# A fused attention and two mixture layers on one core: another order for VectorE and ScalarE in the second MoE, another place for the input's sums and the shares in the first

## The chip, the cores and the metric

The program runs on one core of one Trainium2 chip. Five engines work side by side, each through its own list of instructions in order: TensorE (PE, with its weight loads as PEld), VectorE (DVE), ScalarE (ACT), GpSimd (POOL) and SyncE (SP, which issues most loads). They meet at semaphores. The metric is the device time of one execution in microseconds; lower is better.

## What is computed

Attention within clusters gives x of 1536 tokens by 512. A gated layer and then a mixture of four experts follow:

```python
def _moe_ref(x, w_gate, w_val, w_out):
    g = x @ w_gate                      # 512 x 1536
    return g * sigmoid(g) * (x @ w_val) @ w_out
def _moe2_ref(x, domain_probs, w1, w2):
    p = domain_probs / (domain_probs.sum(-1, keepdims=True) + 1e-09)
    for e in range(4):                  # w1[e]: 512 x 1024, w2[e]: 1024 x 512
        out += p[:, e:e + 1] * (np.maximum(x @ w1[e], 0.0) @ w2[e])
```

## The kernel before

All matrices stay in fp32 accuracy: each operand is split into a high and a low part, and a product is three matmuls (high by high, high by low, low by high). The instructions stand on every engine in the order in which the code issues them; no scheduler moves them.

The tokens form three blocks (`tb` 0, 1, 2) of 512. In both MoEs blocks 0 and 1 are multiplied by a scheme of seven products in place of eight, on sums of blocks of the input (`x_sums`) and of the weights (`block_sums`); block 2 is multiplied plainly. The hidden width is cut into chunks. A generator of side work (weight conversion, sums) advances by `step()`; `work(rate)` sets how far.

**First MoE.** Chunk (1,0) runs `up` (gate and value products, silu) and `down_pair`; chunks (1,1) to (1,10) run `up_fast`, and a `down_pair` after each second one. `weights1` is the side work: it converts weights (`conv`) and makes the sums of x (`x_sums(1)`), for which x of blocks 0 and 1 is first copied whole into `acc` (`x_whole`); `down_pair` of chunk (1,0) then writes its results over `acc`. In chunk (1,5) `share_rows` normalizes the probabilities on DVE (`shares`, L772 to L775).

**Second MoE.** Chunks (2,0) to (2,15), four per expert. (2,0) runs plainly; (2,1) to (2,14) run `up_seven` and `down_seven`, the last one `up_seven` and `down`. In `up_seven` PE fills banks: `pa`, `pb`, `pc` for blocks 0 and 1, `third(key, f)` for block 2. From them DVE and ACT make m1, u2, m5 and t21 (a sum on a full bank, then Relu times the token's share in `relu_p`), their high parts by ACT (`hi`, a cast), their low parts by DVE (`lo`, a subtraction), and the differences of the scheme, `ts[1]` to `ts[4]`, each again as high and low. h11, h12, h21, h22 are the hidden blocks; h12's place holds `ts[4]`. Block 2 passes `relu_l`: Relu into the high part on ACT, the low part on DVE.

In `down_seven` seven products go through two pairs of banks, u and q. A product either starts its pair anew or adds to it. After each, either DVE adds the bank to `acc` (`by_v`), or ACT copies it to a buffer `ev` and POOL issues a DMA that adds it to `acc` (`by_a`). Between them stand four products of block 2 (`last_block`), copied by ACT with the token's share. The first product is copied by ACT (L1120), and the third needs the emptied bank:

```python
product(u, raw, 0, b11, True, by_a(0, 0))        # L1131
product(q, sums, 0, ts[1], True, by_v(1, 1))
rest()                                           # rest of t21, ts[4]
last_block(0)
product(u, sums, 256, ts[2], False, by_v(0, 1))  # L1135
```

The `ev` buffers are five, used in turn, and ACT waits for the DMA that last read one. `share_load` fetches the next expert's shares by SP.

## Time and profile before

| | us |
|---|---|
| runs, median of 3 | 1105.49 (1102.17 to 1106.14) |
| the profiled execution | 1110.94 |
| its span | 1108.7 |
| PE busy | 1051.8 |
| DVE, ACT, POOL busy | 825.5, 623.4, 410.5 |

Attention fills about the first 270 us of the span, the first MoE the time to about 554, the second the rest. The times below are from the span's start. A matmul's row has its modelled duration; since matmuls overlap, the distance between two starts tells what one costs. A wait in brackets is idle time of that engine and the instruction that ended it.

### The profile page before, as it was taken

Reading aid. Unit: us, or ns where it says so; the run is one execution under the profiler, and the core shown is the slowest. Engines: PE = TensorE matmul, PEld = TensorE weight load, DVE = VectorE, ACT = ScalarE, POOL = GpSimd, SP = SyncE. Lnnn points to the kernel's source line nnn. Section 1 sums busy time; section 2 is a strip of 40 time slices with the busy share of each in tenths; the row PEclk is TensorE's granted clock in tenths of the full one; section 3 lists DMA queues with packets and bytes.
Section 4 is the critical chain, followed back from the end, with each engine's and each line's share of the span. In section 5 each row is a group of like instructions: output and inputs, shape, how many; then the busy total and the mean of one; then the engine's idle time right before and its main releaser. Section 6 shows DMA issues by size and latency. Waiting matters only on the chain.

```text
span 1108.7 us, 14805 instructions
## 1 busy us (share of the span) xinstructions
PE 1051.8 (95%) x5051; PEld 846.0 (76%) x5051; DVE 825.5 (74%) x1468; ACT 623.4 (56%) x1200; POOL 410.5 (37%) x455
## 2 busy tenths in 40 slices
PE   9999999999999998999999998889988899888998
PEld 6778888887877887888887776667776677666777
DVE  6788888896788778786776667766677665776665
ACT  6778787886575545554455454444545445444451
POOL 2757777642000010101012454445544444444530
PEclk7999999999999999999999999999999999999999
DMA  7687778432614452525001655446563366634652
GB/s 194 169 186 180 160 178 175 116 93 85 159 58 104 105 115 77 133 65 125 20 20 38 133 114 125 81 100 133 114 139 86 83 130 114 131 75 99 133 95 114
DMA packets 61267, 126.23 MB, mean 114 GB/s; under 512 B 15648, under 2 KB 20256, under 8 KB 61192
## 3 DMA queue, kind: packets, MB, share of 16 engines
q0 software_dynamic: 35632, 62.93, 30.7%
q1 hardware_dynamic: 25272, 62.30, 18.6%
q8 instruction: 39, 0.64, 0.2%
q14 instruction: 36, 0.29, 0.1%
q10 hardware_dynamic: 288, 0.07, 0.0%
HBM read 69.47 MB, written 3.21 MB: 66 GB/s over the span
## 4 chain that ended last, share of the span: by engine, by line
PE 71%; DVE 16%; ACT 6%; issue 3%; DMA 2%; POOL 0%; DVEq 0%; ACTq 0%; SPq 0%; POOLq 0%
PE pa L889 12%; PE pb L266 9%; PE pd L1223 8%; PE pd L1103 8%; PE ps L449 5%; PE pb L1153 4%; PE ps L426 4%; DVE snap L1008 3%; PE pb L889 3%; PE ps L427 3%; PE pa L266 2%; PE pv L479 2%; PE pv L484 2%; PE pc L361 2%; PE pv L485 2%
## 5 line engine op out<-in xcount | busy, mean ns | idle before, releaser
L432 DVE CUSTOM_DVE_ANT_0 junk<-ps,zero 128x768 bf16<-128x768 f32 x96 | 91.0, 947 | 15.6 <-PE ps L427 13.3
L194 POOL TENSOR_TENSOR ws<-wraw 128x256 f32<-128x256 f32 x29 | 35.8, 1235 | 170.7 <-issue 101.2
L1121 POOL DMA_DIRECT2D acc<-ev x84 | 74.4, 1026 | 65.8 <-ACT ev L1120 60.8
L1229 POOL DMA_DIRECT2D acc<-ev x24 | 20.7, 884 | 209.1 <-ACT ev L1228 204.5
L443 ACT ACTIVATE P<-ps,nm 128x768 f32<-128x768 f32 x96 | 86.6, 902 | 16.1 <-DVE nm L432 15.8
L1114 DVE TENSOR_TENSOR acc<-pd,acc 128x512 f32<-128x512 f32 x112 | 74.0, 686 | 19.7 <-PE pd L1103 19.4
L266 PE MATMUL pb<-xh,wuh 128*128 128x512 f32 x216 | 85.4, 396 | 0.0
L266 PE MATMUL pb<-xh,wul 128*128 128x512 f32 x216 | 84.9, 393 | 0.0
L266 PE MATMUL pb<-xl,wuh 128*128 128x512 f32 x216 | 84.1, 389 | 0.0
L449 PE MATMUL ps<-ident,P 128*128 128x128 f32 x576 | 82.7, 275 | 0.0
L468 DVE TENSOR_TENSOR lo<-ps,hi 128x384 fp32r<-128x384 f32 x128 | 69.3, 554 | 15.1 <-ACT hi L454 14.0
L426 PE MATMUL ps<-t 80*128 80x512 f32 x192 | 71.6, 373 | 1.0 <-ACT t L402 0.8
L1129 POOL DMA_DIRECT2D acc<-ev x56 | 50.1, 944 | 60.2 <-ACT ev L1128 46.5
L454 ACT CAST hi<-ps 128x384 fp32r<-128x384 f32 x128 | 57.3, 479 | 20.8 <-PE ps L449 20.4
L889 PE MATMUL pa<-xsh,wuh 128*128 128x512 f32 x150 | 61.2, 408 | 7.7 <-DVE snap L1005 7.4
L449 PEld LDWEIGHTS ps<-ident,P 128*128 128x128 f32 x576 | 65.5, 141 | 1.5 <-DVE lo L468 0.2
L1128 ACT ACTIVATE ev<-pb,pn 128x512 f32<-128x512 f32 x56 | 37.4, 686 | 48.3 <-DMA acc<-ev 35.6
L427 PE MATMUL ps<-t 128*128 128x512 f32 x192 | 63.1, 349 | 0.0
L889 PE MATMUL pa<-xh,wuh 128*128 128x512 f32 x150 | 58.6, 391 | 2.5 <-ACT snap L894 2.5
L889 PE MATMUL pa<-xsh,wul 128*128 128x512 f32 x150 | 59.0, 393 | 0.0
L889 PE MATMUL pa<-xsl,wuh 128*128 128x512 f32 x150 | 58.9, 393 | 0.0
L1223 PE MATMUL pd<-hh,wdh 128*128 128x512 f32 x144 | 56.8, 394 | 2.0 <-ACT acc L1225 2.0
(272 smaller groups left out, 3194.2 us busy)
## 6 DMA issues: line engine op xcount, KB each, us to landing
acc<-ev POOLq DMA_DIRECT2D x164, 256.0 KB, 4.9
wraw<-in_wm SPq DMA_DIRECT2D x68, 512.0 KB, 3.5
t<-in_qk POOLq DMA_DIRECT2D x13, 768.0 KB, 6.1
t<-in_qk POOLq DMA_DIRECT2D x14, 384.0 KB, 6.8
raw<-in_qk SPq DMA_DIRECT2D x26, 192.0 KB, 6.4
x<-x SPq DMA_DIRECT2D x21, 192.0 KB, 2.9
R<-rd SPq DMA_DIRECT2D x16, 192.0 KB, 3.5
out<-acc SPq DMA_DIRECT2D x11, 256.0 KB, 2.0
```

The costliest lines, as they stand in the source:

```text
L266: T.matmul(out=ps, lhsT=w[:, o:o + 128], rhs=x, start=(k == 0 and m == 0), stop=(k == 3 and m == 2))
L426: T.matmul(out=ps, lhsT=t2[:, 0, qs], rhs=t2[:, 1, ks], start=True, stop=False)
L427: T.matmul(out=ps, lhsT=t1[:, 0, qs], rhs=t1[:, 1, ks], start=False, stop=True)
L432: V.tensor_tensor_reduce(out=junk, in0=S_t[n], in1=zero1.to_broadcast([128, S]), scale=-0.125, scalar=3.0e38, op0=ALU.add, op1=ALU.min, ac ...
L443: A.activation(out=P_t[n], in_=S_t.pop(n), func=ACTF.Exp, scale=0.125, bias=nm_t.pop(n), accum_out=rs_t[p][:, h, c:c + 1])
L449: T.transpose(ps[:, i * 128:(i + 1) * 128], P_t[3 * u + i][:, j * 128:(j + 1) * 128], ident)
L468: V.tensor_tensor(out=lo, in0=ps, in1=hi.bitcast(F32), op=ALU.subtract)
L889: T.matmul(out=ps, lhsT=w[:, o:o + 128], rhs=r, start=first and i == 0 and m == 0, stop=i == 1 and m == 2, skip_group_check=not first)
L1103: T.matmul(out=ps[s], lhsT=w[i][:, o + s * 128:o + s * 128 + 128], rhs=x[j], start=first and m == 0, stop=m == 2, skip_group_check=not first)
L1114: V.tensor_tensor(out=y, in0=ps, in1=y, op=ALU.add)
L1121: G.dma_start(out=acc1[:, 2 * half + s, tb * 512:(tb + 1) * 512], in_=ev, accum_op=ALU.add)
L1223: T.matmul(out=ps, lhsT=w[:, o:o + 128], rhs=x[:, f, sl], start=(n == 0), stop=(n == len(terms) - 1))
```

## The change

In the second MoE, the DVE and ACT work of `up_seven` is issued in another order. DVE's sums on banks (`plus`) come ahead of the differences. The Relu of block 2's second half is split: its ACT part (`relu_h`) stays in `up_seven`, its DVE part (`relu_lo`) follows the second product of `down_seven`. t21 and its high part (`c21`) move there too, behind ACT's copies of the first product; the rest of t21 follows the third product. Three steps of side work come ahead of block 2's first half, and the last steps of `down_seven` go.

In the first MoE, the shares are made in chunk (1,0), from a tile that is loaded ahead of x; the sums of x come after two converted pieces of weights in place of four, and wait until block 1 of that chunk has been multiplied; `up` and `down_pair` of that chunk take the blocks in the order 0, 1, 2.

```diff
@@ share_rows
-            pt = ev_.tile([128, 128, E2], F32, tag="ev", name="pt")[0:NR]
-            SY.dma_start(out=pt, in_=probs_t)
-            yield
             shares(ct["pr"], prs[:, 0:NL], pn)
             yield
             to = ev_.tile([128, E2, 128], F32, tag="ev", name="po")[0:NR]
-            shares(pt, prs[0:NR], to.rearrange("t e n -> t n e"))
+            shares(ct["pt"], prs[0:NR], to.rearrange("t e n -> t n e"))
@@ relu_l is split
+        def relu_h(key, f, g):
+            A.activation(out=h_blk(key, f, 2)[0], in_=g, func=ACTF.Relu)
+
+        def relu_lo(key, f, g):
+            h = h_blk(key, f, 2)
+            V.scalar_tensor_tensor(out=h[1], in0=g, scalar=0.0, in1=h[0].bitcast(F32), op0=ALU.max, op1=ALU.subtract)
@@ up_seven
             prod(key, pa, S_(2), T_(2), False)
             u2 = snap(pa)
             lo(h11, m1)
+            for _ in range(3):
+                step()
             relu_l(key, 0, third(key, 0))
-            step()
             prod(key, pc, S_(4), B_(1, 1), False)
             plus(u2, pc, u2)
             relu_p(key, u2, u2, 1)
+            if not blocks:
+                hi(h12, u2)
+            prod(key, pa, S_(3), T_(3), False)
+            plus(m5, pa, m5)
+            relu_p(key, m5, m5, 1)
+            hi(h22, m5)
+            g = third(key, 1)
+            prod(key, pa, A_(1, 1), T_(4), False)
             if blocks:
                 ts[1] = [wp.tile([128, 512], F32R, tag="wb", name="th", bufs=2) for _ in range(2)]
                 minus(m1, u2, m1)
                 hi(ts[1], m1)
-                step()
-                lo(ts[1], m1)
-            else:
-                hi(h12, u2)
-                step()
-                lo(h12, u2)
-            prod(key, pa, S_(3), T_(3), False)
-            plus(m5, pa, m5)
-            relu_p(key, m5, m5, 1)
-            hi(h22, m5)
-            if blocks:
                 minus(u2, m5, u2)
                 hi(ts[3], u2)
                 lo(h22, m5)
                 minus(m5, m5, m1)
+                lo(ts[1], m1)
+                relu_h(key, 1, g)
                 hi(ts[2], m5)
-            else:
-                lo(h22, m5)
-            step()
-            relu_l(key, 1, third(key, 1))
-            if blocks:
                 lo(ts[2], m5)
                 lo(ts[3], u2)
-            prod(key, pa, A_(1, 1), T_(4), False)
...
-            relu_p(key, t21, pa, 0)
-            hi(h21, t21)
+
+            def c21():
+                relu_p(key, t21, pa, 0)
+                hi(h21, t21)
 
             def rest():
                 lo(h21, t21)
                 minus(t21, t21, m5)
                 hi(ts[4], t21)
+                step()
                 lo(ts[4], t21)
@@ down_seven
-            if (key[1] + 1) % NC2 == 0:
-                share_load(e + 1)
...
             product(u, raw, 0, b11, True, by_a(0, 0))
             product(q, sums, 0, ts[1], True, by_v(1, 1))
-            rest()
+            relu_lo(key, 1, g)
+            c21()
+            h_t.pop(key)
+            if (key[1] + 1) % NC2 == 0:
+                share_load(e + 1)
             last_block(0)
             product(u, sums, 256, ts[2], False, by_v(0, 1))
             step()
+            rest()
             product(q, sums, 768, b22, False, by_a(0, 1))
...
             product(q, raw, DM, b21, True, by_v(0, 0))
-            step()
             last_block(2)
             product(u, raw, DM + 256, ts[4], False, by_v(1, 0))
-            step()
             last_block(3)
@@ up
-            for tb in (0, 2, 1):
+            for tb in range(3):
...
+                        done.add((key, f, tb))
@@ down_pair
-            for tb in (1, 0, 2) if last else (2, 0, 1) if first else (1, 2, 0):
+            for tb in (1, 0, 2) if last else (0, 1, 2) if first else (1, 2, 0):
@@ weights1
-            yield from conv(todo[:4])
+            yield from conv(todo[:2])
+            yield from share_rows()
+            while (chunks[0], 1, 1) not in done:
+                yield
             yield from x_sums(1)
-            yield from conv(todo[4:])
+            yield from conv(todo[2:])
@@ the loop over chunks
+        ct["pt"] = ev_.tile([128, 128, E2], F32, tag="ev", name="pt")[0:NR]
+        SY.dma_start(out=ct["pt"], in_=probs_t)
         x_whole()
...
-                work(2.5)
+                work(3)
                 down_pair(k)
```

What this does to the order, at three places. First DVE, in chunk (2,3) of the second MoE, from the sum on the m5 bank (before: from the u2 bank). snap_7319 is u2, snap_7309 m5, snap_7277 m1, th is ts[1], wul holds the low parts of ts[2] and ts[3], pd are the down banks. Before:

```order
L1005 TENSOR_TENSOR snap_7319<-pa_7302,snap_7319 128x512
L996 SCALAR_TENSOR_TENSOR snap_7319<-snap_7319,pe_6288 128x512
L1008 TENSOR_TENSOR snap_7277<-snap_7319,snap_7277 128x512
L250 TENSOR_TENSOR wsl_7294<-ws_7295,wsh_7293 128x512
L1002 TENSOR_TENSOR th_7350<-snap_7277,th_7349 128x512
L1005 TENSOR_TENSOR snap_7309<-pa_7270,snap_7309 128x512
L996 SCALAR_TENSOR_TENSOR snap_7309<-snap_7309,pe_6288 128x512
L1008 TENSOR_TENSOR snap_7319<-snap_7309,snap_7319 128x512
L1002 TENSOR_TENSOR hl_7280<-snap_7309,hh_7279 128x512
L1008 TENSOR_TENSOR snap_7309<-snap_7309,snap_7277 128x512
L250 TENSOR_TENSOR wsl_7294<-ws_7296,wsh_7293 128x512
L1013 SCALAR_TENSOR_TENSOR hl_7280<-pb_7380,hh_7279 128x512
```

Now:

```order
L1002 TENSOR_TENSOR snap_7309<-pa_7270,snap_7309 128x512
L993 SCALAR_TENSOR_TENSOR snap_7309<-snap_7309,pe_6288 128x512
L1005 TENSOR_TENSOR snap_7277<-snap_7319,snap_7277 128x512
L1005 TENSOR_TENSOR snap_7319<-snap_7309,snap_7319 128x512
L999 TENSOR_TENSOR hl_7280<-snap_7309,hh_7279 128x512
L1005 TENSOR_TENSOR snap_7309<-snap_7309,snap_7277 128x512
L999 TENSOR_TENSOR th_7390<-snap_7277,th_7389 128x512
L999 TENSOR_TENSOR wul_7068<-snap_7309,wuh_7067 128x512
L999 TENSOR_TENSOR wul_7068<-snap_7319,wuh_7067 128x512
L1118 TENSOR_TENSOR acc_4134<-pd_7405,acc_4134 128x512
L1118 TENSOR_TENSOR acc_4134<-pd_7406,acc_4134 128x512
L1012 SCALAR_TENSOR_TENSOR hl_7280<-pb_7370,hh_7279 128x512
```

The sum on m5's bank comes ahead of the difference, a weight half and ts[1]'s low part; the sums of the q banks (L1118) come ahead of block 2's low half (L1012).

Second ACT, in the same chunk, around the copies of the u bank (L1120, now L1124). hh<-t21 is first the high part of h21, then that of ts[4]; the last rows named L1120 or L1124 copy the q bank. Before:

```order
L247 CAST wuh_7370<-wraw_7206 128x512
L1012 ACTIVATE hh_7279<-pb_7380 128x512
L999 CAST hh_7279<-t21_7403 128x512
L1120 COPY ev_7417<-pd_7410 128x512
L1120 COPY ev_7423<-pd_7411 128x512
L999 CAST hh_7279<-t21_7403 128x512
L1128 ACTIVATE ev_7445<-pb_7438,pn_74 128x512
L247 CAST wuh_7370<-wraw_7206 128x512
L1120 COPY ev_7461<-pd_7412 128x512
L1120 COPY ev_7467<-pd_7413 128x512
```

Now:

```order
L1008 ACTIVATE hh_7279<-pb_7370 128x512
L996 CAST wuh_7067<-snap_7309 128x512
L1124 COPY ev_7410<-pd_7403 128x512
L1124 COPY ev_7416<-pd_7404 128x512
L996 CAST hh_7279<-t21_7402 128x512
L1132 ACTIVATE ev_7441<-pb_7434,pn_74 128x512
L247 CAST wuh_7328<-wraw_7193 128x512
L996 CAST hh_7279<-t21_7402 128x512
L247 CAST wuh_7328<-ws_7330 128x512
L1124 COPY ev_7465<-pd_7405 128x512
L1124 COPY ev_7471<-pd_7406 128x512
```

Block 2's Relu (L1012, now L1008) moves ahead of a cast, and the u copies move ahead of the first cast of t21; the second cast stays ahead of the q copies.

Third ACT, at the first `down_pair` of the first MoE: L844 are casts of the sums of x, L1225 (now L1233) copies of down banks into acc. Before:

```order
L1225 COPY acc_4134<-pd_4372 128x512
L1225 COPY acc_4134<-pd_4382 128x512
L844 CAST xh_75<-t_4390 128x512
L844 CAST xh_75<-t_4391 128x512
L844 CAST xsh_4142<-t_4396 128x512
L844 CAST xsh_4142<-t_4397 128x512
L844 CAST xsh_4142<-t_4402 128x512
L844 CAST xsh_4142<-t_4403 128x512
L844 CAST xsh_4142<-t_4408 128x512
L1225 COPY acc_4134<-pd_4412 128x512
L844 CAST xsh_4142<-t_4409 128x512
```

Now:

```order
L844 CAST xh_75<-t_4315 128x512
L844 CAST xh_75<-t_4316 128x512
L1205 ACTIVATE sg_4333<-pa_4300 128x512
L1207 CAST hh_4154<-sg_4333 128x512
L844 CAST xsh_4142<-t_4337 128x512
L844 CAST xsh_4142<-t_4338 128x512
L844 CAST xsh_4142<-t_4344 128x512
L844 CAST xsh_4142<-t_4345 128x512
L844 CAST xsh_4142<-t_4350 128x512
L1233 COPY acc_4134<-pd_4354 128x512
L844 CAST xsh_4142<-t_4351 128x512
L1233 COPY acc_4134<-pd_4366 128x512
```

Four copies stood ahead of the sums' casts, those of block 2; now the casts stand ahead of the first copy, which is one of block 0.

## Rows read from the trace of the kernel before

**Rows 1.** The page, busy time of PE: us, share of the span, instructions.

```profile
PE 1051.8 (95%) x5051; PEld 846.0 (76%) x5051; DVE 825.5 (74%) x1468; ACT 623.4 (56%) x1200; POOL 410.5 (37%) x455
```

**Rows 2.** PE's waits, 600 to 1075 us: us in total, times, longest.

```profile
PE pd L1103 <- ACT ev L1120: 34.3, 15, 2.4
PE pa L889 <- DVE snap L1005: 7.4, 14, 0.5
PE pb L889 <- ACT ev L1128: 0.7, 3, 0.3
```

**Rows 3.** Stretches: us, PE busy (matmuls), granted clock, DMA; the third has all engines.

```profile
656.65:690.65 34.00, 31.04 (x134) 1.00 0.57 122
...
861.47:897.54 36.07, 32.95 (x133) 0.95 0.55 111
...
587.10:1073.20 486.10, 443.72 (x1849) 348.93 (x1848) 338.56 (x505) 234.95 (x421) 225.49 (x251) 0.98 0.52 108
...
610.00:613.30 3.30, 3.25 (x8) 0.50 0.49 86
```

**Rows 4.** Timeline of PE in one chunk: start, duration in us, line, operation, wait.

```profile
667.64 0.40 PE L266 MATMUL pb<-xh,wuh 128*128 128x512 f32 x1
...
671.10 0.50 PE L889 MATMUL pa<-xsh,wuh 128*128 128x512 f32 x1 [0.53 <-DVE snap L1005]
...
676.70 0.50 PE L1153 MATMUL pb<-wdh,hl 128*128 128x512 f32 x1
679.63 0.50 PE L1103 MATMUL pd<-wuh,wsh 128*128 128x512 f32 x1 [2.43 <-ACT ev L1120]
```

**Rows 5.** Timeline of ACT in the same chunk.

```profile
678.48 0.62 ACT L999 CAST hh<-t 128x512 fp32r<-128x512 f32 x1 [2.56 <-DVE t L996]
679.00 1.07 ACT L1120 COPY ev<-pd 128x512 f32<-128x512 f32 x2
...
682.61 1.30 ACT L1120 COPY ev<-pd 128x512 f32<-128x512 f32 x2
...
691.11 1.27 ACT L1128 ACTIVATE ev<-pb,pn 128x512 f32<-128x512 f32 x2 [3.15 <-DMA acc<-ev]
```

**Rows 6.** Timeline of DVE in the same chunk.

```profile
666.93 0.68 DVE L1005 TENSOR_TENSOR snap<-pa,snap 128x512 f32<-128x512 f32 x1
667.64 0.69 DVE L996 SCALAR_TENSOR_TENSOR snap<-snap,pe 128x512 f32<-128x512 f32 x1
...
671.80 1.12 DVE L1008 TENSOR_TENSOR snap<-snap 128x512 f32<-128x512 f32 x1
...
675.95 0.69 DVE L1013 SCALAR_TENSOR_TENSOR hl<-pb,hh 128x512 fp32r<-128x512 f32 x1 [1.10 <-ACT hh L1012]
676.56 1.28 DVE L1002 TENSOR_TENSOR wul<-snap,wuh 128x512 fp32r<-128x512 f32 x2
```

**Rows 7.** POOL and SP in the same chunk, and the accumulating DMAs' time to landing.

```profile
671.11 1.26 POOL L195 TENSOR_TENSOR ws<-ws,wraw 128x256 f32<-128x256 f32 x1
...
684.82 0.33 SPq L98 DMA_DIRECT2D wraw<-in_wm  x1
...
DMA to landing us min/median/max: 3.4/5.5/7.1
```

**Rows 8.** PE's waits, 275 to 560 us.

```profile
PE pa L889 <- ACT snap L894: 2.5, 1, 2.5
PE pd L1223 <- ACT acc L1225: 2.0, 1, 2.0
```

**Rows 9.** Timelines of DVE and ACT in the first MoE: chunk (1,0), then chunk (1,5).

```profile
291.09 0.69 DVE L1198 TENSOR_TENSOR sg<-sg,pb 128x512 f32<-128x512 f32 x1 [2.46 <-PE pb L266]
...
429.94 0.16 DVE L772 TENSOR_REDUCE prs<-pr 128x4 f32<-128x16 f32 x1
...
433.62 0.67 DVE L928 TENSOR_TENSOR sg<-pb,snap 128x512 f32<-128x512 f32 x1
...
434.32 0.63 ACT L930 ACTIVATE sg<-sg 128x512 f32<-128x512 f32 x1 [5.50 <-DVE sg L928]
```

More of the change, by code (lines that the diff above doesn't have):

```diff
@@ L1008, in minus @@
             V.tensor_tensor(out=out, in0=x, in1=y, op=ALU.subtract)
+        def relu_h(key, f, g):
[3 more added lines that the diff above has]
+            V.scalar_tensor_tensor(out=h[1], in0=g, scalar=0.0, in1=h[0].bitcast(F32), op0=ALU.max, op1=ALU.subtract)
         def relu_l(key, f, g):
-            h = h_blk(key, f, 2)
-            A.activation(out=h[0], in_=g, func=ACTF.Relu)
-            V.scalar_tensor_tensor(out=h[1], in0=g, scalar=0.0, in1=h[0].bitcast(F32), op0=ALU.max, op1=ALU.subtract)
+            relu_h(key, f, g)
+            relu_lo(key, f, g)
         def h_blk(key, f, tb):
@@ L1063, in up_seven @@
                 minus(m5, m5, m1)
+                lo(ts[1], m1)
+                relu_h(key, 1, g)
                 hi(ts[2], m5)
-            else:
-                lo(h22, m5)
-            step()
-            relu_l(key, 1, third(key, 1))
-            if blocks:
                 lo(ts[2], m5)
                 lo(ts[3], u2)
-            prod(key, pa, A_(1, 1), T_(4), False)
+            else:
+                lo(h12, u2)
+                lo(h22, m5)
+                relu_h(key, 1, g)
+                relu_lo(key, 1, g)
+            wt.pop((key, "u"))
             t21 = tp.tile([128, 512], F32, tag="snap", name="t21", bufs=3)
-            relu_p(key, t21, pa, 0)
-            hi(h21, t21)
-            wt.pop((key, "u"))
+            def c21():
+                relu_p(key, t21, pa, 0)
+                hi(h21, t21)
             def rest():
@@ L1081, in rest, with down_seven @@
                 hi(ts[4], t21)
+                step()
                 lo(ts[4], t21)
             if not blocks:
+                c21()
                 lo(h21, t21)
-            return ts, rest
-        def down_seven(key, ts, rest):
+            return ts, g, c21, rest
+        def down_seven(key, ts, g, c21, rest):
             e = key[1] // NC2
@@ L1092, in down_seven @@
             b11, _, b21, b22 = (h_blk(key, f, tb) for f in range(2) for tb in range(2))
-            h = h_t.pop(key)
+            h = h_t[key]
             raw, sums = wt.pop((key, "d")), wt.pop((key, "s"))
-            if (key[1] + 1) % NC2 == 0:
-                share_load(e + 1)
             u, q = ([down_banks[0].tile([128, 512], F32, tag="d", name="pd") for _ in range(2)] for _ in range(2))
@@ L1132, in down_seven @@
             product(q, sums, 0, ts[1], True, by_v(1, 1))
-            rest()
+            relu_lo(key, 1, g)
+            c21()
+            h_t.pop(key)
+            if (key[1] + 1) % NC2 == 0:
+                share_load(e + 1)
             last_block(0)
@@ L1301, in moe @@
                 work(2)
-                if k[1] == 5:
-                    side_rows = share_rows()
-                    next(side_rows)
                 up_fast(k, chunks[i + 1] if k[1] % 2 else None)
                 done.add((k, "up"))
-                if k[1] == 5:
-                    for _ in side_rows:
-                        pass
                 if k[1] % 2 == 0:
```

## Prediction

> **What bounds the kernel now.** I read the page first. TensorE (PE) is busy 95% of the span and no other engine is above 74% [rows 1]. So a change pays only where PE stands still, and costs only where it makes PE stand still. Next I read who PE waited for, in two stretches. From 600 to 1075 us, the second MoE, three groups hold nearly everything: 34.3 us in 15 waits of up to 2.4 us at the down product, for ScalarE's (ACT's) copy of a bank; 7.4 us in 14 waits of 0.5 us for VectorE's (DVE's) sum on a full bank; 0.7 us at the next chunk's second product [rows 2]. From 275 to 560 us, the first MoE, two waits count: 2.5 us and 2.0 us [rows 8].
>
> Then I read the 14 middle chunks one by one, each from its first matmul to the next chunk's. A good one takes 34.00 us; all 14 take 486.10 us, which is 10.1 us more than 14 good ones [rows 3]. Five of the 14 show a granted clock of 0.95, the others 1.00. In the five, right behind the 2.4 us wait, PE runs for 3.4 us at 0.50 of the full clock, the 1.2 GHz level [rows 3], and each such fall costs half of 3.4, or 1.7 us: 8.5 of the 10.1 us. The half-microsecond waits were never followed by a fall.
>
> Why does the copy come late? In the good chunk, PE ends the last block's first product around 676.9 and starts the next down product at 679.63 [rows 4]. That product needs bank u emptied by ACT. The bank had been full since about 673, but ACT works in order, and ahead of the copies stands the cast of h21, which waited 2.56 us for DVE to make t21 [rows 5]. DVE had a queue: the low half of h(f=1) went at 675.95, two more low halves at 676.56, only then t21 [rows 6]. So the 2.4 us are a queue order, not work.
>
> **The change, second MoE, per chunk.** PE's own order is the same row for row; only DVE's and ACT's orders move. Times are those of the good chunk. One matmul costs 31.04 / 134 = 0.232 us [rows 3].
>
> Bank read first. DVE's sum on the m5 bank now follows the u2 share directly. The u2 sum starts at 666.93, the next dependent one 0.71 us later [rows 6], so the m5 sum stands at about 668.2 and has read its bank by 668.9. PE wants that bank 12 matmuls after 667.64 [rows 4], at 670.4. The 0.53 us wait goes, with 1.5 us to spare.
>
> Copies first. ACT's copies of u now stand behind the cast of ts[2] only. DVE makes ts[2]'s input by about 672.8, ACT casts it to 673.4, and two copies at 0.52 us each (a pair takes 1.07 [rows 5]) end near 674.5. PE could start the next down product 36 matmuls after 667.64, at 676.0. The copies are 1.5 us early: the 2.43 us wait goes.
>
> What is late next. The last block's sixth matmul needs the low half of h(f=1), and that now stands 13 DVE operations behind the u2 sum, two of them sums on banks that used to come later. Four of the steps depend on the one before (0.72 us), nine don't (0.60, half of the pair of 1.28 less its overlap [rows 6]): 4 x 0.72 + 9 x 0.60 = 8.3 us, so it starts at 675.2 and ends at 675.9. On top come collisions with GpSimd (POOL). DVE's subtraction at 671.80 took 1.12 us where its neighbours take 0.69, and it overlapped a POOL sum of weights that ran from 671.11 to 672.37 [rows 6, 7]. The change pulls three weight steps ahead of the third block's Relu, so POOL's four sums for the next chunk start near 666 instead of 669.8 and fall on this very stretch. None of four hits: 675.9. All four: 4 x 0.43 = 1.7 us later, 677.6. I take one, as in the chunk read: 676.3. PE wanted the half at 667.64 + 35 x 0.232 = 675.8, so it waits about 0.6 us, and the next down product starts at 676.6 instead of 679.63: 3.0 us gained, of 3.65 possible.
>
> The Trainium skill speaks to this collision, in "SBUF — State Buffer", section "Who interferes with whom": DVE and GpSimd share a port pair as an exclusive lock, and a DVE operation meets it only with both inputs in SBUF. By that rule the sums on banks are immune, at most two of the exposed operations are hit, and the chunk is 0.4 us longer than by one hit; the one long subtraction, which reads two SBUF tiles, agrees.
>
> What that passes on. The second cast for t21 (the high part of ts[4]) now stands shortly before ACT's copies of bank q, and it waits for DVE: t21, two sums that wait for PE until 677.5, a weight half, the low half of h21, the difference, ending at 680.7. Two casts later the first q copy runs from 681.8 to 682.4. PE wants that bank 24 matmuls after 676.6, at 682.2: a new wait of about 0.5 us with the release. Net gain 3.0 - 0.5 = 2.5, chunk 31.5 us; by the ends above 30.35 (no wait at all) and 32.8 (four hits).
>
> The moved steps also bring two casts and a weight cast ahead of the third block's Relu on ACT, 0.6 us. Its reader, the low half on DVE, used to end 0.5 us before the u2 sum; PE fills u2's bank only just before 666.9, so that cover takes most of it. The weight load on SyncE (SP) went out at 684.82, among the accumulating DMAs of q [rows 7]; it now follows a DVE step at about 681, ahead of them. The share load moves behind the t21 step; its readers come a chunk later.
>
> Clock. The longest wait left is about 0.6 us, of the size never followed by a fall, so I count no falls. The 14 chunks: 14 x 31.5 = 441.0 against 486.1, a gain of 45.1 us.
>
> **The change, first MoE.** The shares: eight small DVE operations, from 429.94 to 433.62 or 3.7 us, stood in front of a sum on a bank, ACT idled 5.50 us for it, and its next copy released PE 2.5 us late [rows 8, 9]. They move to about 291.7, behind a product for which DVE had waited 2.46 us at the same place [rows 9]. Gain 2.5 us; 1.2 us of them is uncovered there and pushes the sums of the input. Those sums and their casts move ahead by about 5 us, but the down blocks now run in the order 0, 1, 2, and the first block's copies overwrite what the sums read: five casts still stand ahead of the first copy. PE filled four banks by 301.9; working the two queues through (silu at 298.5, then five pairs of subtraction and cast at 0.6 us each side) gives the first copy at 304.1. So a 2.2 us wait replaces the 2.0 us one. Between nothing gained and 2.0 + 1.7 for the clock I take 0.8. The input's extra load on SP ahead of x has nothing waiting before 296. First MoE: 3.3 us. The last chunk's edits have no PE wait to remove: 0, within 0.5.
>
> **Sum.** The profiled execution took 1110.94 us (span 1108.7). 1110.9 - 45.1 - 3.3 = 1062.5. The runs' median, 1105.49, lies 5.4 us below it; part of this may be clock falls that I have already removed, so I take 1.5 of it: **1061 us**.
>
> **Rivals.**
> *Landing loop.* The third last-block copy reuses the buffer of the second q copy and waits for its DMA. Before, the q copies ended at 683.9 and that copy started at 691.11, 7.2 us later, at landings of 3.4 to 7.1 us [rows 5, 7]; the next chunk's second product needs its bank. With q copied at 683.0 and an unchanged 7.2 us the bank comes free at 690.9; the next chunk, 2.5 us earlier, wants it at 689.5. A wait of 1.4 us per chunk, chunk 32.9, gain 25.5 + 3.3: 1082. For it: 0.7 us of such waits already stand in the trace [rows 2]. Against: the load that stretched the landings leaves, and u's DMAs go out 5 us earlier; at a landing of 5 us there is no wait.
> *The wait only moves (the change doesn't do what it says).* DVE, busy from 666.9 to the end, comes 2.4 us later still, and PE waits in the last block what it waited behind it, falls included: only the first MoE's 0 to 3, so 1105. Against: the chain above is 8.3 us of counted steps.
> *Slower.* The difference for ts[4] comes 2 us late (collisions and weight halves behind it), so ACT copies q at 685 to 686. Then PE waits over 2.4 us there, the clock falls in some chunks, and the landing of 7.2 us puts the next second product at 693.6 or later: chunk 36, 14 x 36 = 504, or 1126 us. It decides once the q copies end later than about 684.6 in the chunk read; I have them end at 683.0.
>
> **Chances.** Forecast 0.62, landing loop 0.22, moved wait 0.08, slower 0.08. Low end: chunk 30.9, 3.3 us, and 4 us of the offset, 1050. High end: the landing loop with nothing from the sums of the input, 1085. Together these hold 0.84. About 0.5% (5.5 us) is what a measurement of this kernel can tell from no change: faster 0.84, same 0.08, slower 0.08.
>
> **What would show it.** Right: PE's wait for the ACT copy at the down product falls from 34 to under 8 us, the 0.5 us waits for the bank sum are gone, the chunk windows show 31 to 32 us at clock 1.00, a short wait for the low half appears in the first last block, and PE's 2.5 us wait near 437 is gone. Wrong: waits at the next chunk's second product (landing loop), a wait of 2 us or more inside the last block (DVE the bound), POOL sums of 1.2 us beside DVE rows of 1.1 us throughout 666 to 677.

## The result and the profile after

| | before | after |
|---|---|---|
| runs, median | 1105.82 (1102.17 to 1109.33) | **1058.47** (1058.09 to 1058.93) |
| the profiled execution | 1110.94 | 1058.7 |
| its span | 1108.7 | 1056.5 |

The ratio is 0.9572, with an interval of 0.9541 to 0.9604. The prediction said 1061 us. The page after, busy time, answers to [rows 1]:

```profile
PE 1035.0 (98%) x5051; PEld 839.3 (79%) x5051; DVE 819.0 (78%) x1468; ACT 619.0 (59%) x1200; POOL 404.7 (38%) x455
```

The four largest groups of PE's waits, whole span (us in total, times, longest), answer to [rows 2, 8]:

```profile
PE pb L1160 <- DVE hl L1012: 4.9, 14, 0.6
PE pd L1107 <- ACT ev L1124: 4.0, 14, 0.3
PE pd L1231 <- ACT acc L1233: 2.1, 1, 2.1
PE pa L889 <- ACT snap L894: 1.3, 1, 1.3
```

The 34.3 us for the copies of u and the 7.4 us for the sum on a full bank are gone. In their place stand the first two rows, 0.35 and 0.3 us a chunk: the low half of h(f=1) in the first last block, and the copies of q. The stretches, a middle chunk and all 14 (us, five engines' busy time, granted clock, DMA share, GB/s), answer to [rows 3]:

```profile
675.78:707.08 31.30, 30.75 (x134) 24.62 (x132) 23.63 (x36) 16.40 (x31) 15.77 (x18) 1.00 0.58 118
...
581.17:1021.33 440.16, 431.24 (x1850) 344.45 (x1849) 333.23 (x505) 230.14 (x421) 218.62 (x250) 1.00 0.57 118
```

The clock is 1.00 through all 14 chunks. Between the two profiled executions 52.2 us lie: 46.0 in the 14 chunks (486.2 to 440.2), 1.9 in the first MoE, 0.3 behind the chunks, and 4.0 ahead of the first MoE, where the change touches nothing but one load (the last section comes back to them). The first MoE's first matmul starts at 257.62 us in before and at 253.58 in after.

DVE in the same chunk, from the u2 sum to the low half (start, us, line, operation), answers to [rows 6]:

```profile
685.62 0.68 DVE L1002 TENSOR_TENSOR snap<-pa,snap 128x512 f32<-128x512 f32 x1
686.34 1.10 DVE L993 SCALAR_TENSOR_TENSOR snap<-snap,pe 128x512 f32<-128x512 f32 x1
687.36 0.68 DVE L1002 TENSOR_TENSOR snap<-pa,snap 128x512 f32<-128x512 f32 x1
...
691.34 0.68 DVE L999 TENSOR_TENSOR th<-snap,th 128x512 fp32r<-128x512 f32 x1
692.11 1.29 DVE L999 TENSOR_TENSOR wul<-snap,wuh 128x512 fp32r<-128x512 f32 x2
693.32 1.28 DVE L1118 TENSOR_TENSOR acc<-pd,acc 128x512 f32<-128x512 f32 x2
694.52 0.68 DVE L1012 SCALAR_TENSOR_TENSOR hl<-pb,hh 128x512 fp32r<-128x512 f32 x1
```

The m5 sum follows 1.74 us behind the u2 sum instead of 3.43, and the low half starts 8.90 us behind it. One operation is long, 1.10 instead of 0.69 us, beside these rows of POOL:

```profile
686.15 0.74 POOL L197 TENSOR_TENSOR ws<-wraw 128x256 f32<-128x256 f32 x1
686.85 1.19 POOL L198 TENSOR_TENSOR ws<-wraw,ws 128x256 f32<-128x256 f32 x1
```

ACT: the copies of u stand early, those of q behind the second cast of t21, and the third last block's copy behind a landing [rows 5]:

```profile
691.98 1.12 ACT L1124 COPY ev<-pd 128x512 f32<-128x512 f32 x2
...
699.82 0.62 ACT L996 CAST hh<-t 128x512 fp32r<-128x512 f32 x1 [2.27 <-DVE t L1005]
...
700.87 1.06 ACT L1124 COPY ev<-pd 128x512 f32<-128x512 f32 x2
...
706.75 0.69 ACT L1132 ACTIVATE ev<-pb,pn 128x512 f32<-128x512 f32 x1 [2.74 <-DMA acc<-ev]
```

SP's weight load, and the landings of the four accumulating DMAs of line L1125 that follow it (two of q, then two of u's third product, issued 701.7 to 704.4), answer to [rows 7]:

```profile
700.48 0.33 SPq L98 DMA_DIRECT2D wraw<-in_wm  x1
```

```profile
DMA to landing us min/median/max: 3.4/5.0/6.4
```

And PE's two waits of that chunk, then its two of the first MoE, [rows 4, 8]:

```profile
695.25 0.50 PE L1160 MATMUL pb<-wdh,hl 128*128 128x512 f32 x1 [0.26 <-DVE hl L1012]
701.50 0.50 PE L1107 MATMUL pd<-hh,wdh 128*128 128x512 f32 x1 [0.29 <-ACT ev L1124]
...
299.99 0.50 PE L1231 MATMUL pd<-hh,wdh 128*128 128x512 f32 x1 [2.13 <-ACT acc L1233]
...
318.55 0.51 PE L889 MATMUL pa<-xsh,wuh 128*128 128x512 f32 x1 [1.33 <-ACT snap L894]
```

### The profile page after: what moved, and what is told of

It reads as the page before. It is cut to its first block, busy times and chain, and to the rows that moved or that the text cites. A ratio compares the mean times of both kernels' runs of the same rounds, so it can differ in the third digit from the quotient of the medians.

```text
span 1056.5 us, 14774 instructions
## 1 busy us (share of the span) xinstructions
PE 1035.0 (98%) x5051; PEld 839.3 (79%) x5051; DVE 819.0 (78%) x1468; ACT 619.0 (59%) x1200; POOL 404.7 (38%) x455
## 4 chain that ended last, share of the span: by engine, by line
PE 70%; DVE 17%; ACT 10%; issue 3%; DMA 0%; ACTq 0%; DVEq 0%; SPq 0%
PE pa L889 10%; PE pd L1231 8%; PE pd L1107 7%; PE pb L266 7%; PE pb L1160 6%; PE ps L449 6%; PE ps L426 4%; DVE snap L993 3%; PE pb L889 3%; PE ps L427 3%; DVE snap L1005 3%; DVE snap L1002 3%; PE pv L479 2%; PE pa L266 2%; PE pv L484 2%
## 5 line engine op out<-in xcount | busy, mean ns | idle before, releaser
L1125 POOL DMA_DIRECT2D acc<-ev x84 | 80.0, 1185 | 117.0 <-ACT ev L1124 116.5
L1237 POOL DMA_DIRECT2D acc<-ev x24 | 20.6, 867 | 205.2 <-ACT ev L1236 205.2
L1118 DVE TENSOR_TENSOR acc<-pd,acc 128x512 f32<-128x512 f32 x112 | 74.6, 687 | 21.8 <-PE pd L1107 21.8
L1133 POOL DMA_DIRECT2D acc<-ev x56 | 51.2, 978 | 61.8 <-DVE acc L1118 35.4
L996 ACT CAST hh<-snap 128x512 fp32r<-128x512 f32 x31 | 19.3, 621 | 93.3 <-DVE snap L993 93.3
L996 ACT CAST hh<-t 128x512 fp32r<-128x512 f32 x33 | 20.5, 622 | 77.3 <-DVE t L993 45.4
```

The source lines that it names most:

```text
L1118: V.tensor_tensor(out=y, in0=ps, in1=y, op=ALU.add)
L1125: G.dma_start(out=acc1[:, 2 * half + s, tb * 512:(tb + 1) * 512], in_=ev, accum_op=ALU.add)
```

## The experiments

The change to the second MoE has three parts: **B**, DVE reads the full banks first; **C**, the copies of u ahead of t21; **S**, the steps of side work in other places. The table tells for each kernel when four things start, in us after the start of the u2 sum (median of its 14 chunks), and what PE waits for in a chunk. e1 and e10 are built on the kernel before, the others on the change, with its first MoE (2 us).

| kernel | us | th low | low half | t21 | u copies | PE waits |
|---|---|---|---|---|---|---|
| before | 1105.8 | 2.82 | 9.02 | 10.83 | 12.07 | u copies 2.4, bank 0.5 |
| C (e1) | 1101.5 | 2.82 | 10.97 | 11.56 | 8.89 | low half 1.9, bank 0.5 |
| S (e10) | 1101.6 | 3.28 | 8.59 | 10.40 | 11.65 | u copies 1.9, bank 0.9 |
| B, C (e9) | 1101.5 | 8.12 | 11.30 | 11.90 | 8.76 | th low 2.2, low half 0.6 |
| B, C, no POOL sums (e11) | 1067.1 | 6.52 | 9.69 | 10.29 | 7.16 | th low 0.6, low half 0.6 |
| B, S (e2) | 1057.5 | 5.86 | 6.47 | 8.27 | 9.51 | u copies 0.6 |
| B, C, S (after) | 1058.5 | 5.71 | 8.90 | 9.50 | 6.36 | low half 0.35, q 0.3 |
| the same, no POOL sums (e12) | 1071.7 | 5.38 | 8.93 | 9.53 | 6.29 | low half 0.25, q 0.3, next pb 0.8 |
| low half ahead of q sums (e5) | 1045.2 | 5.72 | 7.70 | 9.49 | 6.36 | none in most |

From start and wait follow three limits: when each must start for PE not to wait. The low part of th (ts[1]): 8.12 - 2.2 and 6.52 - 0.6, both 5.9 us. The low half, with the waits ahead of it taken off as well: 8.90 - 0.35, 10.97 - 1.9 - 0.5 and 11.30 - 0.6 - 2.2, 8.5 to 8.6 us. The u copies: 9.51 - 0.6, 11.65 - 1.9 - 0.9 and 12.07 - 2.4 - 0.5, 8.9 to 9.2 us. A chunk without a wait meets all three. Two of the eight combinations of the parts were not run: B alone, and C with S.

**e1: the copies ahead, alone** (C, on the kernel before).

```diff
-            relu_l(key, 1, third(key, 1))
+            g = third(key, 1)
+            relu_h(key, 1, g)
...
-            relu_p(key, t21, pa, 0)
-            hi(h21, t21)
...
             product(q, sums, 0, ts[1], True, by_v(1, 1))
-            rest()
+            relu_lo(key, 1, g)
+            c21()
             last_block(0)
             product(u, sums, 256, ts[2], False, by_v(0, 1))
             step()
+            rest()
```

> The kernel before, with one part of the change: the low half of block 2, t21 and the rest of t21 move behind ScalarE's copies of the first product, as in the change; VectorE's order inside up_seven, the steps of side work and the first MoE stay as before. Theory (one VectorE queue feeds both waits, so the two parts overlap): the bank wait of 0.53 us stays, the copy wait goes, but block 2's low half now comes about 1.65 us late, since it stands behind the two bank sums in a queue that is already long; chunk 32.7 us, hardly a clock fall, about 1077 us. Rival (each part is worth the wait it is named for): the whole 34.3 us and the falls behind it go, 43 us gained, about 1063 us.

Measured: 1101.48 us, ratio 0.9987 (0.9966 to 1.0007). Neither theory had the time. The first had the waits right (the bank wait stays, the copy wait goes, the low half is late, by 1.9 us where 1.65 were expected) and the chunk wrong: 34.3 us on average (479.7 / 14) instead of 32.7. PE's waits, 275 to 1075 us:

```profile
PE pb L1167 <- DVE hl L1015: 27.0, 14, 1.9
PE pa L889 <- DVE snap L1005: 7.4, 14, 0.5
PE pb L889 <- ACT ev L1137: 5.2, 10, 0.9
```

The wait of 2.4 us for the copies became one of 1.9 us for the low half, and behind three of these the clock fell. The copies came 3.2 us sooner; the low half came 2 us later.

**e2: the change without C** (B and S).

```diff
                 relu_h(key, 1, g)
+                relu_lo(key, 1, g)
...
+            c21()
             if not blocks:
-                c21()
...
-            relu_lo(key, 1, g)
-            c21()
             h_t.pop(key)
+            rest()
...
             step()
-            rest()
```

> The changed kernel, with the other part taken back: VectorE still reads full banks ahead of the sums and the steps stand as in the change, but block 2's low half, t21 and its high part stay in up_seven ahead of ScalarE's copies, and the rest of t21 follows the second product. Theory (one queue): t21 now stands only 12 VectorE operations behind the u2 sum and ends near 675.7 in the good chunk's times, its cast near 676.3, the first copy near 676.85 against 676.0 wanted: a wait of 0.9 us in place of 2.4, chunk 32.0 us, no falls, about 1068 us. Rival (each part is worth its own wait): only 7.4 us of the second MoE go and the copy wait of 2.4 us stays with its falls, about 1096 us.

Measured: 1057.46 us, ratio 0.9588 (0.9551 to 0.9624), the time of the whole change. PE's waits, 275 to 1075 us:

```profile
PE pd L1108 <- ACT ev L1125: 10.1, 15, 1.9
```

That is 0.6 us a chunk at the copies of u, as much as the full change waits at two other places; the one of 1.9 us is a copy that itself waited 4.07 us for a landing, in the chunk that starts at 923.4. The theory named the right place, but with 0.9 us and 1068 us it had it too dear; the rival, 1096 us, is out. C is worth nothing once B and S are there, and by e1 nothing without them.

**e9: the change with the steps at their old places** (B and C).

```diff
-            for _ in range(3):
-                step()
             relu_l(key, 0, third(key, 0))
+            step()
...
             relu_p(key, u2, u2, 1)
+            step()
...
             hi(h22, m5)
+            step()
...
                 hi(ts[4], t21)
-                step()
...
             product(q, raw, DM, b21, True, by_v(0, 0))
+            step()
             last_block(2)
             product(u, raw, DM + 256, ts[4], False, by_v(1, 0))
+            step()
```

> The changed kernel with the steps of side work back at their old places in the second MoE. Theory (VectorE's chain from the u2 sum to block 2's low half sets the wait in the last block): two weight halves of 0.6 us return into the chain, one collision with GpSimd of 0.4 us leaves it, so block 2's low half comes 0.8 us later; chunk 32.1 us, about 1069 us. Rival (the steps are only shifted and cost nothing): 1058 us. Second rival (GpSimd's sums in the chain are what costs): faster than 1058, about 1052 us.

Measured: 1101.51 us, ratio 0.998 (0.9955 to 1.0005). No theory had the size, nor the place: the low half was expected to bind. PE's waits, 275 to 1075 us:

```profile
PE pd L1107 <- DVE th L999: 30.8, 14, 2.2
PE pb L1162 <- DVE hl L1012: 6.1, 10, 0.6
PE pb L889 <- ACT ev L1132: 5.0, 10, 1.8
```

A wait that was in neither kernel: the second product waits for th, which B had moved from 2.82 to behind the m5 sum. DVE in one chunk, whose u2 sum started at 733.61:

```profile
734.94 0.69 DVE L250 TENSOR_TENSOR wsl<-ws,wsh 128x512 fp32r<-128x512 f32 x1
...
736.97 1.23 DVE L250 TENSOR_TENSOR wsl<-ws,wsh 128x512 fp32r<-128x512 f32 x1
738.12 1.83 DVE L1005 TENSOR_TENSOR snap<-snap 128x512 f32<-128x512 f32 x2
739.87 1.22 DVE L999 TENSOR_TENSOR hl<-snap,hh 128x512 fp32r<-128x512 f32 x1
741.12 0.69 DVE L1005 TENSOR_TENSOR snap<-snap 128x512 f32<-128x512 f32 x1
741.73 0.68 DVE L999 TENSOR_TENSOR th<-snap,th 128x512 fp32r<-128x512 f32 x1
```

and POOL beside it:

```profile
738.27 1.12 POOL L197 TENSOR_TENSOR ws<-wraw 128x256 f32<-128x256 f32 x1 [0.63 <-DVE wsl L250]
739.36 1.18 POOL L198 TENSOR_TENSOR ws<-wraw,ws 128x256 f32<-128x256 f32 x1
```

Two halves of weights (L250) stand in the chain again, and POOL's sums run beside a weight half, the differences and a low half: 1.23, 1.83 for a pair (1.41 in after), 1.22. th starts at 8.12 instead of 5.71, past its limit of 5.9.

**e10: the steps, alone** (S, on the kernel before).

```diff
+            for _ in range(3):
+                step()
             relu_l(key, 0, third(key, 0))
-            step()
...
                 hi(ts[1], m1)
-                step()
...
                 lo(h22, m5)
-            step()
             relu_l(key, 1, third(key, 1))
...
                 hi(ts[4], t21)
+                step()
...
             product(q, raw, DM, b21, True, by_v(0, 0))
-            step()
             last_block(2)
             product(u, raw, DM + 256, ts[4], False, by_v(1, 0))
-            step()
```

> The kernel before, in which only the steps of the side work are moved to where the change has them (three ahead of the first third() of a chunk, one in rest(), none after the two products that now have none). VectorE's order of bank reads, the order of the copies and the first MoE are those of before. Theory 1, the steps carry the gain alone: two halves of weights and the POOL sums beside them leave VectorE's chain to hh<-t, the 2.43 us wait for the copy at the u banks shrinks to under 0.5 us, the bank wait of 0.53 us stays; a chunk takes 31.5 to 32.2 us and the kernel 1064 to 1074 us. Theory 2, the steps help only together with the new bank order (in the old order the low parts still stand ahead of th and of the copies): the copy wait keeps 1.2 us or more, a chunk takes 32.8 us or more, the kernel 1083 to 1100 us.

Measured: 1101.64 us, ratio 0.9948 (0.9919 to 0.9978); theory 2, though a little beyond its range. PE's waits, 560 to 1075 us:

```profile
PE pd L1102 <- ACT ev L1119: 28.1, 15, 1.9
PE pa L889 <- DVE snap L1005: 12.2, 14, 1.3
```

Two of DVE's rows in a chunk tell why the shorter queue does not help in the old order:

```profile
666.45 0.69 DVE L1002 TENSOR_TENSOR th<-snap,th 128x512 fp32r<-128x512 f32 x1 [0.69 <-ACT th L999]
...
671.76 0.69 DVE L1013 SCALAR_TENSOR_TENSOR hl<-pb,hh 128x512 fp32r<-128x512 f32 x1 [1.18 <-ACT hh L1012]
```

At the first, where a weight half stood, DVE now waits 0.69 us for ACT's cast, which in turn waits for DVE's difference. The second wait stood in before too (1.10 us behind a weight half, [rows 6]) and is 1.18 us without it. So of the 1.2 us of two weight halves 0.4 are left: t21 comes at 10.40 instead of 10.83, the u copies at 11.65 instead of 12.07. B puts other work of the chain into those gaps; with it (e2) the same steps bring t21 at 8.27.

**e11: e9 without POOL's sums.** As in e9, and

```diff
-                *_, sums = block_sums(G, *a)
+                sums = [raw[:, j * 512:(j + 1) * 512] for j in range(2)]
```

> The full change with the steps at their old places (as in the run with old steps, 1101.5 us), and without POOL's sums of weight quarters: the slices of the raw weights stand where the sums stood, so the products that use sums compute something else. The casts and low parts of the weights are as many as before; only POOL's work beside VectorE is gone. Theory A, collisions of VectorE with POOL make the wait of 2.2 us at the u copies: some three collisions of 0.4 us leave the chain, the wait falls to about 1.0 us, the falls of the clock go with it, and the kernel takes 1075 to 1086 us. Theory B, the two halves of weights that stand in the chain make the wait: it stays at 1.8 us or more and the kernel takes 1093 us or more.

Measured: 1067.07 us, ratio 0.9631 (0.9572 to 0.969). PE's waits, 560 to 1075 us:

```profile
PE pd L1107 <- DVE th L999: 8.3, 14, 0.6
PE pb L1162 <- DVE hl L1012: 8.3, 14, 0.6
```

Theory A, and more of it than expected (the wait of 2.2 us that it names is the one for th, not one at the u copies): th starts 1.6 us sooner (8.12 to 6.52), with the two weight halves still in the chain and every operation there at 0.69 us. So of the 2.4 us by which e9's th is later than the change's, 1.6 are POOL; the other 0.8 are two halves at 0.6, less the one collision of 0.4 that the change itself has.

**e12: the change without POOL's sums.** The same edit on the full change.

> The full change without POOL's sums of weight quarters (slices of the raw weights stand in their place, so the products that use sums compute something else). Theory, the prediction's step (c): the one long VectorE operation behind the u2 sum (1.10 instead of 0.69 us) is a collision with POOL and makes most of the wait for the low half of h(f=1) in the last block; without POOL's sums it takes 0.69 us, the wait of 0.35 us falls to under 0.1, a chunk takes 30.8 to 31.0 us and the kernel 1051 to 1055 us. Rival: the length of that operation has another cause, or the wait passes on whole to the copies of q; chunk 31.3 us and 1057 to 1060 us.

Measured: 1071.73 us, ratio 0.9704 (0.9671 to 0.9737), slower than the change. Both theories missed (their "step (c)" is the prediction's paragraph on what is late next). PE's waits, 275 to 1075 us:

```profile
PE pb L889 <- ACT ev L1132: 10.9, 13, 1.6
PE pd L1107 <- ACT ev L1124: 4.0, 14, 0.3
PE pb L1160 <- DVE hl L1012: 3.5, 14, 0.2
```

The long operation is gone (0.69 us where the change has 1.10), so that was POOL. The wait for the low half fell from 0.35 to 0.25 only, because next in the chain the sums on the q banks wait for PE (0.19 us), and the low half still starts 8.93 us behind the u2 sum. But the first row is the landing loop of the prediction. Without the sums the raw weights are read by the last steps, so SP's next load goes out later, in one chunk at 704.58, right when DVE's last half of raw weights ends (703.86 and 0.69). SP, the landings of the same four DMAs (L1125, issued 703.1 to 705.8) and ACT there:

```profile
704.58 0.33 SPq L98 DMA_DIRECT2D wraw<-in_wm  x1
```

```profile
DMA to landing us min/median/max: 3.2/6.4/7.6
```

```profile
709.65 1.26 ACT L1132 ACTIVATE ev<-pb,pn 128x512 f32<-128x512 f32 x2 [4.27 <-DMA acc<-ev]
```

In the change the load went out 1.3 us ahead of q's first DMA and they landed in a median of 5.0 us; here it goes out between them, the median is 6.4 us, ACT waits 4.27 us for a landing, and PE for ACT. That it is the load and not the missing sums shows in the last of e12's 14 chunks, which has no load there; its four DMAs (issued from 1027.5) land as in the change:

```profile
DMA to landing us min/median/max: 3.2/4.8/6.6
```

**e8: three buffers for the copies instead of five.**

```diff
-            evs = itertools.cycle((ev_, tp))
+            evs = itertools.cycle((tp,))
```

> The changed kernel with three buffers for the copies of down banks in place of five. Measures how near the landing loop is, the rival of the prediction. If the loop is near: a copy waits for the DMA of the third copy before it; the second u copies wait for the landing of the q copies, 2.3 us late, the next product 1.5 us, and the third last block's bank comes free after the next chunk's second product wants it; chunk 34 to 35 us with falls of the clock, 1095 to 1108 us. If landings have several us to spare: no more than 1065 us.

Measured: 1099.78 us, ratio 0.996 (0.9933 to 0.9986): as expected for "near". The copies wait for landings (45.2 us in 28 waits), and PE for the copies, 275 to 1075 us:

```profile
PE pd L1107 <- ACT ev L1124: 31.7, 42, 2.2
```

With two buffers fewer nearly the whole gain is gone: the landings have no several us to spare. With all five buffers they still cost PE next to nothing when both present waits go (e5 below: 0.8 us in 3 waits at the next chunk's second product).

**e3 and e4: one MoE of the change at a time.** e3 is the change with the first MoE of before, e4 the kernel before with the first MoE of the change; in short, for e3:

```diff
-            for tb in range(3):
+            for tb in (0, 2, 1):
...
-            yield from conv(todo[:2])
-            yield from share_rows()
-            while (chunks[0], 1, 1) not in done:
-                yield
+            yield from conv(todo[:4])
             yield from x_sums(1)
```

> The changed kernel with the first MoE of the kernel before (shares in chunk (1,5), sums of x after four converted pieces, blocks in the old order). By the two traces the first MoE from its first down product to its end takes 258.2 us before and 256.3 now, so the theory expects 1060.4 us, with the 2.5 us wait near 437 back and a wait of about 2 us at the first down product either way. Rival (the first MoE's edits give the 3.3 us that were forecast, or more): 1062 or more.

> The kernel before with the first MoE of the changed kernel alone. Theory: 1.9 us under the kernel before, within what falls of the clock scatter, ratio about 0.998. Rival: the first MoE is worth 4 us or more, ratio under 0.996.

Measured: e3 1060.85 us, ratio 0.9619 (0.9596 to 0.9642); e4 1106.21 us, ratio 1.0007 (0.9982 to 1.0032). Both are as expected (1060.4 us; about 0.998). By time the first MoE's part can't be told from nothing. By the traces it can: from the first matmul of the first down stage to the first of chunk (2,0)'s down stage it takes 274.5 us in before and e3, and 272.6 in after and e4.

**e5, e6, e7: what is left.** e5 puts the low half ahead of the sums on the q banks and t21's rest behind the copies of q; e6 puts ACT's casts of the input's sums next to DVE's low parts; e7 does both.

```diff
-            product(q, sums, 0, ts[1], True, by_v(1, 1))
             relu_lo(key, 1, g)
+            product(q, sums, 0, ts[1], True, by_v(1, 1))
             c21()
...
-            rest()
             product(q, sums, 768, b22, False, by_a(0, 1))
+            rest()
@@ x_sums (e6)
-                    A.copy(out=x_sum(i)[j][0], in_=t)
+                    if n == 2:
+                        A.copy(out=x_sum(i)[j][0], in_=t)
                     yield
...
+                    if n == 1:
+                        A.copy(out=hi, in_=t)
+                        yield
```

> The changed kernel with both waits that are left in the second MoE attacked: block 2's low half goes ahead of the two q bank sums on VectorE, and the rest of t21 behind the copies of q. Theory: the waits of 0.4 us for the low half and 0.45 us for the q copies go in each of 14 chunks, about 0.8 us each, chunk 30.5 us, about 1047 us. Rival (VectorE's queue is full, so the wait moves to the product that needs ts[4] or to the landing loop): half of it, about 1053 us, or nothing.

> The changed kernel with the casts of the sums of x in the first MoE moved behind the subtractions, next to the low parts, so that they don't stand ahead of ScalarE's first copies of down banks. Theory (casts ahead of the first copy make the wait of 2.1 us, and the clock falls behind it): the first copy then waits only for VectorE's sixth subtraction, about 1 us earlier, the wait halves and the fall goes, about 1055 us. Rival (VectorE's subtractions bound the first copy, or the casts come late for the next chunk): 1058 us.

> The full change with both additions: the low half of h(f=1) ahead of the sums on the q banks and the t21 rest behind the copies of q, and the casts of the input's sums next to their low parts. If the two gains add (13.2 us in the second MoE, 2 us in the first), 1042 to 1045 us; if the first MoE's 2 us were scatter between runs, 1045 to 1047 us.

Measured: e5 1045.22 us, ratio 0.9474 (0.9451 to 0.9498); e6 1056.54, ratio 0.9577 (0.9552 to 0.9602); e7 **1039.99**, ratio 0.9404 (0.9382 to 0.9426), faster than both kernels. In e5 the low half starts at 7.70, within its limit, and of PE's waits in the second MoE no group over 1 us is left, as the theory had it (1047 us). e6's gain is within scatter by time; by the traces the first MoE's stretch of 272.6 us takes 269.2 in e6 and e7, 3.4 us less, which is the wait of 2.1 us and the new one of 1.3 us, both gone. e7 came out under both of its expectations (1042 us and more). A chunk of e7:

```profile
728.63:758.79 30.16, 30.16 (x133) 24.78 (x132) 23.98 (x36) 16.34 (x30) 15.68 (x18) 1.00 0.61 122
```

## Why the prediction came out right, step by step

**The bank wait of 0.5 us** went, as worked out. e9 and e2 have B in common and neither has that wait; e1 and e10 lack B and keep it.

**The copy wait of 2.4 us** went, and the u copies stand where the prediction put them: their pair ends 7.5 us behind the u2 sum, predicted 7.6. But the reason given, that they stand ahead of t21, is not what the gain hangs on. e2 leaves them behind t21 and is as fast, since with B and S t21 itself comes 2.6 us sooner (8.27 instead of 10.83).

**The low half** was the best sized term: 13 operations, 8.3 us and one collision of 0.43 made 8.7 us, measured 8.90. PE's wait is 0.35 us instead of 0.6. In part this is luck: the collision was counted as the one thing between 8.3 and 8.7, but without any collision (e12) the low half still starts at 8.93, since the sums on the q banks then wait for PE, a bound that the prediction did not have for them. **The wait at the q copies** was predicted at 0.5 and is 0.3. Together a chunk of 31.5 us, and 441.0 us for the 14; measured 31.3 to 32.0, and 440.2. No fall of the clock, as counted.

**The moved steps** are the step that failed. The prediction priced them as three operations on ACT, 0.6 us, covered; that side held. What it did not see is what they take out. B moves th from 2.82 to 5.71 us, and PE wants it by 5.9: 0.2 us to spare. With the steps at their old places two weight halves and 1.6 us of collisions stand ahead of it, and the rest of the change is worth nothing (e9). The sum came out right because the chain of 13 operations was counted in the order of the changed kernel, where the weight halves were already gone; the credit was put down to B and C alone. By the runs it belongs to B and S together: e2 has it without C, e9 (B and C) and e10 (S alone) don't have it. B alone was not run; that it gives nothing is argued from e9, whose wait for th stands ahead of everything that C moves. C with S was not run either, so what those two would give without B stays open.

**The collisions.** One was taken, one is there. The page "SBUF — State Buffer" of the Trainium skill, section "Who interferes with whom", says that a DVE operation with at most one SBUF input, outside the two-port modes, does not contend with GpSimd, and that one with two SBUF inputs contends with a GpSimd operation that reads SBUF. The traces agree: beside POOL's rows the sums on banks keep 0.68 us (685.62, 687.36), the long ones of e9 all read two SBUF tiles, and without POOL's sums all take 0.69 (e11, e12). The bound of two hits held for the change's order, not for e9's, where three operations are long.

**The landing loop** did not come, for the reason given against it: SP's load now goes out ahead of q's DMAs. e12 puts it back among them and has the loop, with chunks of 32.4 us on average (421.8 / 13, the last 13) where the rival's price was 32.9. It takes late copies of q as well: in e5 the load goes out among them too, but q's first DMA goes out 3.5 us sooner in the chunk than in the change, and PE hardly waits. "At a landing of 5 us there is no wait" fits as well: the median is 5.0 in after and 6.4 in e12.

**"The wait only moves"** was a chance of 0.08 at 1105 us. For the whole change it did not come; for its parts it did: 1101.5 us with the wait at the low half (C alone), at th (B and C) and still at the copies (S alone).

**The first MoE** was put at 3.3 us and gave 1.9 by the trace. The 2.5 us for the shares are gone. The input's sums gave nothing where 0.8 was taken: a wait of 2.1 us stands where 2.0 stood (the prediction's own working had 2.2), with a fall of the clock behind either. The fall in after costs nothing there, where the prediction allowed 1.7: in e4 and e5, which have no fall behind this wait, PE waits 1.65 us more at the next block, and the stretch is as long. And a wait of 1.3 us that nobody had foreseen came at 318.55, where an ACT copy of a bank stands behind a weight conversion. That leaves 2.5 - 0.1 - 1.3 = 1.1 of 1.9. Of the other 0.8, 0.5 are three short waits of before (0.19, 0.07 and 0.25 us) that after does not have; the rest was not traced.

**The sum.** What the change touches was put at 45.1 + 3.3 = 48.4 us and gave 46.0 + 1.9 + 0.3 = 48.2 in the traces. The rest of the 52.2 is the 4.0 us ahead of the first MoE, for which the prediction had taken 1.5 off. One bound does not follow from its own terms: the landing loop with nothing from the sums of the input is 1110.9 - 25.5 - 2.5 = 1082.9 us, not 1085.

## What to carry to other kernels

When several engines hand work round in a ring, write down for each result when it is wanted and when it comes, all from one common event; a reordering that frees one result can push another past its limit, and then the edits pay only together. Work that is "only side work" must be counted by what it stands in front of in the order it has and in the order it had, not by its own length. And before a transfer's buffers or issue time are touched, look at which accumulating transfers will be under way beside it.

## What the runs showed of the hardware that was not expected

DVE's operations on two SBUF tiles grew by 0.4 to 0.5 us each beside POOL's sums, and how many are hit between the u2 sum and the low half goes with the order: one in every chunk of the change (1.04 to 1.21 us), three in every chunk of e9 (1.23, one of a pair of 1.83, 1.22), none without POOL's sums. It is not the order alone: in e10 six of the 14 chunks have two hits and the others one. Taking POOL's sums out of e9 was worth 34 us of 1101.5.

A weight load of 512 KB issued among the accumulating DMAs moved their median landing from 4.8 us (e12's chunk without one) to 6.4 us; issued 1.3 us ahead of them it left it at 5.0 (after).

Of the 14 waits of 1.9 us in e1 three were followed by 3.4 us at a granted clock of 0.50, the 1.2 GHz level; the waits of 0.6 us and the one of 1.3 us of after were followed by none. And the profile of before shows 13.7 us at that level early in attention, behind a first rise at 5.8 us:

```profile
9.00:22.70 13.70, 13.31 (x50) 9.69 (x49) 7.60 (x17) 8.73 (x16) 2.35 (x5) 0.51 1.02 217
```

In other kernels here such a stretch was 13.7 us again (e4), 10.2 us or 3.4 us, with no edit near it; in after, e1, e8 and e11 there is none, but there the clock first rises at 13.6 to 14.0 us. The rows of after name no clock before that; its warm-up matmuls start 0.32 us apart up to 12.4 us, and 0.16 us apart behind 14.5, as those of before do at a granted 1.00 (8.5 to 9.0 us). By this, before ran 5.8 + 13.7 = 19.5 us at the lower level and after 14.0. The 5.5 us more cost about half, an estimate of 2.7 of the 4.0 us by which before's first MoE started later; at the 300th matmul (56.11 and 53.96 us) before is 2.2 us late. Where the rest is lost, and what decides when the clock rises, stays open.
